# In-place activation sums on GpSimd, and three of seven out-projection products one step earlier, in a fused RWKV and feed-forward kernel

## The chip, the cores and the metric

The kernel runs on one core of a Trainium2 chip, in float32. The metric is the device time of one execution in microseconds (us), the median over repeated runs. The five engines run side by side, each through its own queue in order: TensorE (PE in the profile) multiplies matrices, VectorE (DVE) and ScalarE (ACT) compute element by element, GpSimd (POOL) does the same on data in SBUF, SyncE (SP) issues most DMAs. They wait for each other through semaphores.

## The reference

Two blocks in a row: a linear attention with a decaying state (RWKV-6), and a feed-forward layer with the activation h * erf(softplus(h)).

```python
def _attn_ref(r, k, v, w, u):                      # B, H, S, D = 4, 8, 768, 48
    for t in range(S):
        cur = np.einsum('bhd,bhe->bhde', u[None] * kt, vt)
        y[:, :, t] = np.einsum('bhd,bhde->bhe', rt, state + cur)
        state = wt[:, :, :, None] * state + np.einsum('bhd,bhe->bhde', kt, vt)

def _moe_ref(x, w_in, w_out):                      # 3072 x 384, 384 x 2048, 2048 x 384
    h = x @ w_in
    sp = np.maximum(h, 0.0) + np.log1p(np.exp(-np.abs(h)))
    g = h * erf(sp)
    return g @ w_out
```

The attention's output, with batch and sequence as tokens and the heads side by side, is the x of the second block.

## The kernel before

**Units and steps.** The 3072 tokens are cut into 12 units of 256: two batches by 128 positions. Units and steps are counted from 0, so unit 3 is the fourth. Step s does the attention of unit s, the hidden product (x @ w_in) of unit s - 1, the activation of units s - 1 and s - 2, and the out-projection (g @ w_out) of unit s - 3. After step 4 (DIRECT) the steps have one form, `attend_late`; steps 6 to 10 are alike. The last two units share a hidden product of another kind behind step 11.

**Hidden product.** `hidden` yields eight pieces a unit (L1123). A piece takes a PSUM tile from the pool ps_m, multiplies two blocks of 128 hidden features (three matmuls of 256 columns each), and ScalarE copies the tile to h (L1132). Two pieces make a chunk of the activation: softplus and erf on ScalarE (L1079, L1083), a multiplication in place on DVE (L1088).

**Out-projection.** A unit's activations are four quarters: a11 and a12 are the first batch's rows for the first and second half of the 2048 hidden features, a21 and a22 the second batch's. `project_fast` forms the product of this 2 x 2 block matrix and the equally cut w_out with seven products instead of eight (Winograd's form of Strassen's scheme). The sums of weights were made once. The sums of activations are s1 = a21 + a22, s2 = s1 - a11, s3 = a11 - a21, s4 = a12 - s2. `blend` makes them on DVE (L1222 to L1228), s3 in place of a21, the others into free room, and `to_lane` has ScalarE copy a22, a11 and a12 into PSUM first (L1203), so that DVE reads one operand from there. Each product is eight matmuls of 192 columns (L1245) into one of two PSUM tiles m0 and m1. These come from ps_m too, which has two buffers in all: while an out-projection is under way, no hidden piece can begin, and the first hidden piece behind it gets m0's buffer once all readers of m0 are done, the next m1's. The last reader of m0 is DVE's sum into both halves of o[1] (L1265), that of m1 DVE's sum into o[0] (L1270); then SP sends the outputs.

**Order.** The order on each engine is written out by hand. `attend_late` calls the stages front, near, 0, 1, 2, 3, 4 in between its own work, and each stage is a string of tokens: P one product of unit s - 3, Q one product of unit s - 2, H one hidden piece of unit s - 1, s and e one softplus and one erf, m one multiplication, F a part of the next unit's preparation, k a copy to PSUM, S a sum of activations. `LATE` holds the strings of steps 5 and 11, `USUAL` those of 6 to 10:

```python
USUAL = (
    "s P", "m", "ey P m s P P ep P", "m k22y P F P k11p F F", "S1", "S2 S3 H k12y S4 H F",
    "s H ey m H H F s H ep H H",
)
```

**Around it.** A step starts on PE with the own part of the unit before (L673) and one level of the present unit (L641); the stage front follows, then L673 and the part through the state (L699), whose result ScalarE copies and SP moves into xT (L707, L728, L734), the input of the next hidden product. Then `prepare(s + 1)` begins: POOL makes the totals of decays (L408, L430 to L432), a faded state (L802), and its share of the near part: totals L456, fading L463, products L504. DVE takes the rest: L485, L488, L494, L535, L538, the reductions L529, fadings L463. The two wait for each other several times; the first time DVE waits is at L488, for POOL's L463. The stages near and 0 come behind most of that on DVE's queue, so stage 0's multiplication (L1088), kT's scaling (L807) and everything behind them do too. PE's L641 of the last level and L761 stand between stages 0 and 1, the state's update (L748) between 1 and 2.

Of the kernel before, what the change touches and what calls it, by code (L numbers as in the profile page):

```python
# [11 lines left out]
FP32 = mybir.dt.float32  # L12
# [3 lines left out]
ALU = mybir.AluOpType  # L16

P = 128
FAST = 3
SEVEN = 1  # L20
EP = 64
HC = 64
NC = 2
NJ = 2
FG = 8
# [37 lines left out]
def kernel(  # L63
# [14 lines left out]
    nc = tc.nc  # L78
    PSUM = bass.MemoryType.PSUM

    n_steps, _, _, JP, C = rkw.shape
# [4 lines left out]
    _, NT, DM = w_out.shape  # L86
# [3 lines left out]
    SPC = NB // NJ  # L90
    assert C == P == NC * HC and HC == 1 << LOG and NE == 2 and D <= EP and NP * NE * D == DM == KT * P
    assert n_steps == SPC * n_pairs and NP == KT + 1 == 4 and NG == 2 and P // NEAR * NH == P
# [7 lines left out]
    outs = ctx.enter_context(tc.tile_pool(name="outs", bufs=2))  # L100
# [3 lines left out]
    ps_m = ctx.enter_context(tc.tile_pool(name="ps_m", bufs=2, space=PSUM))  # L104
# [19 lines left out]
    w_out_sb = const.tile([P, NT, DM], FP32, name="w_out_sb")  # L124
    ND = DM // NJ
    mixed = const.tile([P, 3, FG, ND], FP32, name="mixed")
# [7 lines left out]
    def products(shape, n=None):  # L134

        if n is None:
            n = turns["next"]
            turns["next"] = 1 - n
        names = "abc"[: len(shape) - 1]
        return banks[n][:].rearrange(  # L140
            f"p ({' '.join(names)}) -> p {' '.join(names)}", **dict(zip(names, shape[1:]))
        )
# [164 lines left out]
    def rows(e, n=D):  # L307
        return slice(e * EP, e * EP + n)

    both = slice(0, EP + D)  # L310

# [375 lines left out]
    def through_state(s, xT):  # L687
# [42 lines left out]
        for kk in range(KT):  # L730
            n = D // KT
            for e in range(NE):
                queue = nc.scalar if (kk, e) in by_scalar else nc.sync
                queue.dma_start(  # L734
                    out=xT[e * EP + D : (e + 1) * EP, kk, :],
                    in_=y3[e * EP + kk * n : e * EP + (kk + 1) * n, :],
                )
# [18 lines left out]
    def spread_blocks(s, pp):  # L756
# [3 lines left out]
        for e in range(NE):  # L760
            nc.tensor.matmul(  # L761
                pp[:EP, e, 0:2, HC // 2 : HC // 2 + n],
                lhsT=over_blocks[rows(e)].rearrange("p b n -> p (b n)"),
# [308 lines left out]
    def lane(kind):  # L1072

        if kind == "y":
            return y[:].rearrange("p e q j t -> p (e q j t)")
        return products([P, NE * JP * HC], 1)[:]

    def softplus_chunk():
        nc.scalar.activation(sp_room, chunks[0], AF.Softplus)  # L1079
# [6 lines left out]
    def multiply_chunk():  # L1086
        h, at = started.pop(0)
        nc.vector.tensor_mul(h, h, at)  # L1088
# [107 lines left out]
    def quarter(of, what):  # L1196

        g, j = int(what[1]) - 1, int(what[0]) - 1
        return gated[of][g][:, :, j * C : (j + 1) * C]

    def to_lane(of, what, kind):
        lanes[what] = lane(kind).rearrange("p (f t) -> p f t", t=C)
        nc.scalar.copy(lanes[what], quarter(of, what))  # L1203

    def blend(of, *parts):
# [14 lines left out]
        for part in parts or (1, 2, 4, 3):  # L1220
# [6 lines left out]
            else:  # L1227
                nc.vector.tensor_sub(s4, a["12"], s2)  # L1228

    def project_fast(s, gs):  # L1230

        c, i = divmod(s, SPC)
        a11, a12, a22 = gs[0][:, :, :C], gs[1][:, :, :C], gs[1][:, :, C:]
        s1, s2, s3, s4 = blends[s]
        upper, lower = w_out_sb[:, :FG], w_out_sb[:, FG:]
        b11, t1, b21, b22 = (x[:, :, k * ND : (k + 1) * ND] for x in (upper, lower) for k in range(2))
        t3, t2, t4 = (mixed[:, n] for n in range(3))
        o = [outs.tile([P, DM], FP32, name="o") for _ in range(NJ)]
        m0 = ps_m.tile([P, DM], FP32, name="m")
        m1 = ps_m.tile([P, DM], FP32, name="m")  # L1240
        lo, hi = slice(0, ND), slice(ND, DM)

        def product(to, a, b, start):
            for f in range(FG):
                nc.tensor.matmul(  # L1245
                    to, lhsT=a[:, f], rhs=b[:, f], start=start and f == 0, stop=f == FG - 1,
                    skip_group_check=True,
                )

        product(m0[:, lo], a11, b11, True)  # L1250
        nc.scalar.copy(o[0][:, lo], m0[:, lo])  # L1251
        yield
        product(m1[:, lo], a22, t4, True)
        yield
        product(m1[:, hi], s1, t1, False)
        nc.scalar.copy(o[1][:], m1[:])
        yield
        product(m0[:, lo], s2, t2, False)
        nc.scalar.copy(o[0][:, hi], m0[:, lo])
        yield  # L1260
        product(m1[:, hi], s4, b22, False)
        yield
        product(m0[:, lo], s3, t3, False)
        halves = o[1][:].rearrange("p (k n) -> p k n", k=2)
        nc.vector.tensor_add(halves, halves, m0[:, None, lo].to_broadcast([P, 2, ND]))  # L1265
        nc.sync.dma_start(out=out[i * NJ + 1, c], in_=o[1][:])
        yield
        if s < n_steps - 1:
            product(m1[:, lo], a12, b21, True)
            nc.vector.tensor_add(o[0][:], o[0][:], m1[:])  # L1270
            nc.sync.dma_start(out=out[i * NJ, c], in_=o[0][:])
        else:
            last = products([P, NE * JP * HC], 0)[:, lo]
            for part, m in ((hi, m1[:, hi]), (lo, last)):
                if m is last:
                    product(m, a12, b21, True)
                nc.vector.tensor_add(o[0][:, part], o[0][:, part], m)
                nc.sync.dma_start(out=out[i * NJ, c, :, part], in_=o[0][:, part])
        yield
# [113 lines left out]
    gated = [[] for _ in range(n_steps)]  # L1393

    def advance(count=None):

        while later and count != 0:
            stage, last = later.pop(0)
            stage()
            count = count and count - 1  # L1400
            if last and not count:
                break
# [10 lines left out]
    def piece(kind, of):  # L1413
        if not 0 <= of < n_steps:
            return
        if of not in kind:
            if kind is hids:
                kind[of] = hidden(of, xTs[of], gated[of], not of)
            else:
                kind[of] = (project_fast if of >= SEVEN else project)(of, gated[of])  # L1420
        next(kind[of])

    def in_order(s, k):
# [8 lines left out]
    STAGES_LATE = ("front", "near", 0, 1, 2, 3, 4)  # L1432
    LATE = {
        DIRECT + 1: (
            "s P", "m", "ey P m P s P ep P", "P m k22y F P k11p", "S1 F F",
            "S2 S3 H k12y S4 H F", "s H ey m H H F s H ep H H",
        ),
        n_steps - 1: (
            "s P", "m w", "ey P m s P P ep P", "m P P", "", "", ""
        ),  # L1440
    }
    USUAL = (
        "s P", "m", "ey P m s P P ep P", "m k22y P F P k11p F F", "S1", "S2 S3 H k12y S4 H F",
        "s H ey m H H F s H ep H H",
    )

    def run_late(s, tokens, following=None):

        for what in tokens.split():
            if what == "A":  # L1450
                advance()
            elif what == "P":
                piece(projs, s - 3)
            elif what == "H":
                piece(hids, s - 1)
            elif what == "F":
                next(following, None)
            elif what == "Q":
                piece(projs, s - 2)
            elif what == "J":  # L1460
                next(turns["joint"])
            elif what == "w":
                next(joining)
            elif what in "uvz":
                activate_pair(what)
            elif what == "T":
                join_tokens()
                turns["joint"] = hidden_of_two()
            elif what == "f":
                turns.pop("fill")()  # L1470
            elif what == "s":
                softplus_chunk()
            elif what[0] == "e":
                erf_chunk(what[1])
            elif what == "m":
                multiply_chunk()
            elif what[0] == "k":
                to_lane(s - 2, what[1:3], what[3])
            else:
                blend(s - 2, *(int(n) for n in what[1:]))  # L1480
                for name in {"S3": ("11", "22"), "S4": ("12",)}.get(what, ()):
                    lanes.pop(name, None)
# [24 lines left out]
    for kk in range(KT):  # L1507
        n = D // KT
        to, of = (x.rearrange("p (e m) -> p e m", e=NE) for x in (apart[:, kk], ident[:]))
        nc.vector.tensor_copy(out=to[:, :, D:], in_=of[:, :, kk * n : (kk + 1) * n])  # L1510
    load_first()
    with tc.manual_schedule(
# [78 lines left out]
        s = n_steps  # L1591
        from_own(s - 1, ready[s - 1][0], 1)
        fence()
        run_late(s - 1, "S Q w w w")
        from_own(s - 1, ready[s - 1][0], 0)
        through_state(s - 1, xTs[s - 1])
        run_late(s, "P P P P T")
        run_late(s, "J J J J J u J u u J")
        run_late(s, "J u v J J v J z z J v v J z u u u J z")
        run_late(s, "J u v J J v J z z J v v J z u u J z")  # L1600
        run_late(s, "J J u v J J z v J z v J z u v J z P P S s ey")
        run_late(s + 1, "P P m s ep P P m P P P S")
        run_late(s + 2, "P P P P P P P")

# [95 lines left out]
```

## Time and profile before

| What | us |
|---|---|
| median of three runs (575.89 to 577.66) | 576.53 |
| span of the profiled execution, first to last instruction | 575.4 |
| from one step's start to the next, steps 6 to 9 | 44.3 |
| of it the hidden product on PE | 20.9 |
| DVE busy in such a step | 37.1 |
| ScalarE busy in such a step | 29.2 |
| GpSimd busy in such a step | 22.6 |

The span is that of one execution taken by the profiler; the runs' times are taken around the whole launch. A row of the timeline gives the start and the duration in us, the engine, the source line, the operation, the tile written and those read, the shape and how many instructions are merged; in brackets, how long the engine had been idle and who released it. A float32 matmul shows as two records, so eight matmuls are x16. Busy matmuls overlap in the records, so PE's pace is read from start to start.

### The profile page before, as it was taken

Reading aid. Unit: us, or ns where it says so; the run is one execution under the profiler, and the core shown is the slowest. Engines: PE = TensorE matmul, PEld = TensorE weight load, DVE = VectorE, ACT = ScalarE, POOL = GpSimd, SP = SyncE. Lnnn points to the kernel's source line nnn. Section 1 sums busy time; section 2 is a strip of 40 time slices with the busy share of each in tenths; the row PEclk is TensorE's granted clock in tenths of the full one; section 3 lists DMA queues with packets and bytes.
Section 4 is the critical chain, followed back from the end, with each engine's and each line's share of the span. In section 5 each row is a group of like instructions: output and inputs, shape, how many; then the busy total and the mean of one; then the engine's idle time right before and its main releaser. Section 6 shows DMA issues by size and latency. Waiting matters only on the chain.

```text
span 575.4 us, 16716 instructions
## 1 busy us (share of the span) xinstructions
PE 568.1 (99%) x7336; PEld 503.9 (88%) x7336; DVE 442.7 (77%) x475; ACT 358.0 (62%) x488; POOL 244.7 (43%) x265
## 2 busy tenths in 40 slices
PE   8999999999999999999999999999999999999997
PEld 6688777678998998998998998998898899988997
DVE  7785887999899998798699699599599527255640
ACT  3668777645458858748747756766766661388700
POOL 4567381632885883393384284185173000000000
PEclk9999999999999999999999999999999999999999
DMA  7595662350435325155145145234232201000000
GB/s 263 192 348 214 240 205 68 161 164 3 147 84 168 109 66 171 21 176 166 18 159 167 32 145 172 40 121 162 39 120 74 48 8 37 1 1 2 27 28 27
DMA packets 54081, 63.24 MB, mean 110 GB/s; under 512 B 35160, under 2 KB 40568, under 8 KB 52984
## 3 DMA queue, kind: packets, MB, share of 16 engines
q1 hardware_dynamic: 53624, 61.98, 34.0%
q8 instruction: 57, 0.93, 0.7%
q10 hardware_dynamic: 384, 0.20, 0.1%
q14 instruction: 16, 0.13, 0.1%
HBM read 52.39 MB, written 8.69 MB: 106 GB/s over the span
## 4 chain that ended last, share of the span: by engine, by line
PE 93%; DVE 4%; ACT 2%; issue 1%; POOL 0%; DVEq 0%; ACTq 0%; POOLq 0%
PE m L1245 34%; PE m L1123 33%; PE pp L641 5%; PE pp L1333 4%; PE m L1155 4%; PE y L1333 2%; PE y L673 2%; PE y L699 2%; PE pp L748 2%; PE m L951 1%; DVE in L334 1%; PE pp L960 1%; PE pp L1033 1%; DVE h L1088 1%; ACT rest L267 0%
## 5 line engine op out<-in xcount | busy, mean ns | idle before, releaser
L1123 PE MATMUL m<-xT,w_in_sb 128*128 128x256 f32 x960 | 215.0, 382 | 0.9 <-ACT h L1132 0.7
L1123 PEld LDWEIGHTS m<-xT,w_in_sb 128*128 128x128 f32 x960 | 179.8, 190 | 26.5 <-ACT h L1132 1.4
L334 DVE TENSOR_TENSOR in<-in,tot_sb 128x1024 f32<-128x1024 f32 (+1 forms) x55 | 80.1, 1457 | 12.7 <-PE pp L641 11.4
L1132 ACT COPY h<-m 128x512 f32<-128x512 f32 x80 | 46.1, 580 | 48.5 <-PE m L1123 48.4
L1245 PE MATMUL m<-mixed,h 128*128 128x192 f32 x320 | 56.7, 331 | 0.0
L1245 PE MATMUL m<-w_out_sb,h 128*128 128x192 f32 x320 | 56.2, 329 | 0.0
L1245 PEld LDWEIGHTS m<-mixed,h 128*128 128x128 f32 x320 | 51.8, 190 | 1.0
L1245 PE MATMUL m<-w_out_sb,room 128*128 128x192 f32 x304 | 52.5, 326 | 0.0
L1245 PEld LDWEIGHTS m<-w_out_sb,h 128*128 128x128 f32 x320 | 52.0, 190 | 0.5
L1245 PEld LDWEIGHTS m<-w_out_sb,room 128*128 128x128 f32 x304 | 49.9, 190 | 0.0
L1083 ACT ACT_TABLE_LOAD x30 | 38.5, 1283 | 10.7 <-DVE h L1088 8.5
L463 POOL TENSOR_TENSOR words<-words,own 128x384 f32<-128x384 f32 x21 | 30.1, 1432 | 22.8 <-DVE words L494 13.0
L504 POOL TENSOR_TENSOR words<-words 128x384 f32<-128x384 f32 x28 | 39.7, 1447 | 0.0
L1079 ACT ACT_TABLE_LOAD x30 | 38.5, 1283 | 1.8 <-issue 1.3
L641 PEld LDWEIGHTS pp<-in 48*48 48x48 f32 (+4 forms) x2368 | 30.1, 120 | 10.8 <-issue 3.5
L456 POOL TENSOR_TENSOR own<-rest 128x384 f32<-128x384 f32 x7 | 9.7, 1379 | 61.0 <-ACT o L1251 61.0
L641 PE MATMUL pp<-in 48*48 48x32 f32 (+4 forms) x2368 | 33.9, 206 | 0.2 <-DVE in L334 0.2
L504 POOL TENSOR_TENSOR rk<-words 128x384 f32<-128x384 f32 x28 | 33.4, 1220 | 0.0
L529 DVE TENSOR_REDUCE sums<-rk 128x16 f32<-128x768 f32 (+2 forms) x31 | 31.6, 1020 | 0.0
L408 POOL TENSOR_TENSOR tot_sb<-tot_sb 128x256 f32<-128x256 f32 (+4 forms) x50 | 28.8, 576 | 3.8
L1079 ACT ACTIVATE room<-h 128x1024 f32<-128x1024 f32 x28 | 29.6, 1057 | 0.3
L1245 PE MATMUL m<-mixed,room 128*128 128x192 f32 x160 | 27.7, 327 | 0.0
(206 smaller groups left out, 981.6 us busy)
## 6 DMA issues: line engine op xcount, KB each, us to landing
in<-in_rkw SPq DMA_DIRECT2D x8, 1024.0 KB, 5.2
words<-in_moe_w_in SPq DMA_DIRECT2D x16, 384.0 KB, 5.4
words<-in_moe_w_out SPq DMA_DIRECT2D x16, 384.0 KB, 5.2
words<-in_rk_rows SPq DMA_DIRECT2D x8, 768.0 KB, 6.1
w<-in_rkw SPq DMA_DIRECT2D x11, 512.0 KB
v<-in_v SPq DMA_DIRECT2D x12, 384.0 KB, 5.6
out<-o SPq DMA_DIRECT2D x23, 192.0 KB, 3.0
in<-in_rkw SPq DMA_DIRECT2D x7, 512.0 KB, 5.6
```

The source lines that it names most:

```text
L334: nc.vector.tensor_mul(halves, halves, view(tots[level - 1], 0, [[1, n], [2, nb], [0, half]]))
L408: nc.gpsimd.tensor_mul(new, pair[:, :, 0], pair[:, :, 1])
L463: engine.tensor_mul(to, to, of[:, :, None, :].to_broadcast([P, NEAR // 2 // half, half, D]))
L504: engine.tensor_mul(to[:, i], r[:, half:], k[:, part * rows + i, None].to_broadcast([P, half, D]),)
L529: nc.vector.tensor_reduce(out=to, in_=of, axis=mybir.AxisListType.X, op=ALU.add)
L641: nc.tensor.matmul(to, lhsT=rk(1, n)[rows(e), s0 : s0 + m], rhs=right, start=True, stop=True,)
L1079: nc.scalar.activation(sp_room, chunks[0], AF.Softplus)
L1083: nc.scalar.activation(at, sp_room, AF.Erf)
L1123: nc.tensor.matmul(ps[:, ff, :], lhsT=w_in_sb[:, g * FG + f + ff, kk * P : (kk + 1) * P], rhs=xT[:, kk, :], start=kk == 0, stop=kk == KT - 1,)
L1132: nc.scalar.copy(h[:, f : f + FT, :], ps[:])
L1245: nc.tensor.matmul(to, lhsT=a[:, f], rhs=b[:, f], start=start and f == 0, stop=f == FG - 1, skip_group_check=True,)
L1333: nc.tensor.matmul(to[:, e], lhsT=a[:, 2 * i + e], rhs=b, start=start and not k, stop=True, skip_group_check=True,)
```

## The change

A new function `project_placed` takes the place of `project_fast` for units 3 to 9 (the last two keep the old form), with a new order of the seven products and another grouping of the same sums. The four sums of activations are made by GpSimd, each in place of a quarter that no later product needs (`blend_placed`, token I). The copies to PSUM (token k) and DVE's sums (token S) go from these units. The first three products (a11, a22, a12 as they are) become tokens Q at the end of the step before, the other four stay in the stages front and 0. The hidden pieces move the other way: one to the end of stage 0, two into stage 1. Steps 5 and 11 and the tail are fitted to it.

```diff
+    def blend_placed(of, part):
+        a11, a12, a21, a22 = (quarter(of, what) for what in ("11", "12", "21", "22"))
+        out_, a, b, op = {
+            3: (a21, a11, a21, ALU.subtract), 2: (a22, a22, a21, ALU.subtract),
+            1: (a11, a11, a22, ALU.add), 4: (a12, a12, a22, ALU.subtract),
+        }[part]
+        nc.gpsimd.tensor_tensor(out=out_, in0=a, in1=b, op=op)
+
+    def project_placed(s, gs):
...
+        product(m0[:, lo], a11, b11, True)
+        nc.scalar.copy(o[0][:, lo], m0[:, lo])
+        yield
+        product(m1[:, lo], a22, t4, True)
+        yield
+        product(m1[:, hi], a12, b21, False)
+        nc.scalar.copy(o[1][:, lo], m1[:, lo])
+        nc.vector.tensor_add(o[0][:, lo], o[0][:, lo], m1[:, hi])
+        yield
+        product(m0[:, lo], a22, t2, False)
+        nc.scalar.copy(o[0][:, hi], m0[:, lo])
+        yield
+        product(m1[:, lo], a11, t1, True)
+        nc.scalar.copy(o[1][:, hi], m1[:, lo])
+        yield
+        product(m0[:, lo], a21, t3, False)
+        halves = o[1][:].rearrange("p (k n) -> p k n", k=2)
+        nc.vector.tensor_add(halves, halves, m0[:, None, lo].to_broadcast([P, 2, ND]))
+        nc.sync.dma_start(out=out[i * NJ + 1, c], in_=o[1][:])
+        yield
+        product(m1[:, lo], a12, b22, False)
+        nc.vector.tensor_add(o[0][:, hi], o[0][:, hi], m1[:, lo])
+        nc.sync.dma_start(out=out[i * NJ, c], in_=o[0][:])
+        yield
...
     LATE = {
         DIRECT + 1: (
-            "s P", "m", "ey P m P s P ep P", "P m k22y F P k11p", "S1 F F",
-            "S2 S3 H k12y S4 H F", "s H ey m H H F s H ep H H",
+            "s P", "m", "ey P m P s P ep P", "P m F P", "I3 F F",
+            "H H F", "s H ey m H H F s H ep H H Q Q I2 Q I1 I4",
         ),
         n_steps - 1: (
-            "s P", "m w", "ey P m s P P ep P", "m P P", "", "", ""
+            "s P", "m w", "ey P m s P ep P", "m I3 Q Q I2", "", "", ""
         ),
     }
     USUAL = (
-        "s P", "m", "ey P m s P P ep P", "m k22y P F P k11p F F", "S1", "S2 S3 H k12y S4 H F",
-        "s H ey m H H F s H ep H H",
+        "s P", "m", "ey P m s P P ep H", "m H F H F F", "I3", "H H F",
+        "s H ey m H H F s Q ep Q I2 Q I1 I4",
     )
...
-        run_late(s - 1, "S Q w w w")
+        run_late(s - 1, "Q I1 I4 w w w")
         from_own(s - 1, ready[s - 1][0], 0)
         through_state(s - 1, xTs[s - 1])
-        run_late(s, "P P P P T")
+        run_late(s, "P P P T")
...
-        run_late(s, "J J u J J z v J z v J z u v J z P P S s ey")
+        run_late(s, "J J u J J z v J z v J z u v J z P S s ey")
```

More of the change, by code (lines that the diff above doesn't have):

```diff
@@ L20 @@
 SEVEN = 1
+PLACED = 3
 EP = 64
@@ L1228, in blend, with product @@
                 nc.vector.tensor_sub(s4, a["12"], s2)
+    def blend_placed(of, part):
[6 more added lines that the diff above has]
+    def project_placed(s, gs):
+        c, i = divmod(s, SPC)
+        a11, a12, a21, a22 = (quarter(s, what) for what in ("11", "12", "21", "22"))
+        upper, lower = w_out_sb[:, :FG], w_out_sb[:, FG:]
+        b11, t1, b21, b22 = (x[:, :, k * ND : (k + 1) * ND] for x in (upper, lower) for k in range(2))
+        t3, t2, t4 = (mixed[:, n] for n in range(3))
+        o = [outs.tile([P, DM], FP32, name="o") for _ in range(NJ)]
+        m0 = ps_m.tile([P, DM], FP32, name="m")
+        m1 = ps_m.tile([P, DM], FP32, name="m")
+        lo, hi = slice(0, ND), slice(ND, DM)
+        def product(to, a, b, start):
+            for f in range(FG):
+                nc.tensor.matmul(
+                    to, lhsT=a[:, f], rhs=b[:, f], start=start and f == 0, stop=f == FG - 1,
+                    skip_group_check=True,
+                )
+        product(m0[:, lo], a11, b11, True)
[22 more added lines that the diff above has]
+        yield
     def project_fast(s, gs):
@@ L1419, in piece @@
             else:
-                kind[of] = (project_fast if of >= SEVEN else project)(of, gated[of])
+                kind[of] = (
+                    project if of < SEVEN
+                    else project_placed if PLACED <= of < n_steps - 2
+                    else project_fast
+                )(of, gated[of])
         next(kind[of])
@@ L1478, in run_late @@
                 to_lane(s - 2, what[1:3], what[3])
+            elif what[0] == "I":
+                blend_placed(s - 2, int(what[1]))
             else:
@@ L1600 @@
         run_late(s, "J u v J J v J z z J v v J z u u J z")
-        run_late(s, "J J u v J J z v J z v J z u v J z P P S s ey")
+        run_late(s, "J J u v J J z v J z v J z u v J z P S s ey")
         run_late(s + 1, "P P m s ep P P m P P P S")
```

## The prediction

> **What bounds the kernel now.** I read the page's busy shares first, then what TensorE (PE) waits for, then one late step instruction by instruction on PE, VectorE (DVE) and GpSimd (POOL). The page says that PE is the busy engine:
>
> ```profile
> PE 568.1 (99%) x7336; PEld 503.9 (88%) x7336; DVE 442.7 (77%) x475; ACT 358.0 (62%) x488; POOL 244.7 (43%) x265
> ```
>
> The list of PE's waits has only two entries over 0.6 us (engine, line, releaser, total, times, longest), one before the first matmul and one for ScalarE's copies of the hidden products:
>
> ```profile
> PE m L951 <- POOL ident masks.py:199: 1.7, 1, 1.7
> PE m L1123 <- ACT h L1132: 0.7, 2, 0.3
> ```
>
> From about 50 us on PE stops once, for 0.35 us at 224.4, and a late step is exactly as long as its matmuls. PE's timeline of the step that begins at 365.63 (start, duration, instruction):
>
> ```profile
> 365.63 0.66 PE L673 MATMUL y<-own,v 64*48 64x64 f32 x32
> ...
> 371.21 2.87 PE L1245 MATMUL m<-mixed,h 128*128 128x192 f32 x16
> 373.92 2.76 PE L1245 MATMUL m<-w_out_sb,room 128*128 128x192 f32 x16
> 376.52 2.76 PE L1245 MATMUL m<-mixed,room 128*128 128x192 f32 x16
> 379.12 2.76 PE L1245 MATMUL m<-w_out_sb,room 128*128 128x192 f32 x16
> ```
>
> The step before began at 321.33: the period is 44.30 us. I count from a step's start, t = 0 at 365.63. An out-projection product is 2.60 to 2.71 us. A piece of the hidden product is 2.62 (96 records in 20.99 us, eight pieces). There is no slack on PE: every wait that the change puts into its queue is paid in full, and nothing on another engine can be won.
>
> **What it takes away.** Per unit four DVE sums (1.21 us each) and three ScalarE copies (1.02) go. Both lie wholly under PE's 44.30 us, so they are worth 0. The one wait that they cause, the 0.35 us in step 5 (a copy of the hidden product stands behind them on ScalarE), may go: -0.35 us. PE's work stays seven products a unit. The smaller copies out of PSUM (ScalarE two of 192 columns for one of 384, DVE one of 192 more) are 0.3 us each on engines with room: 0. The same two output DMAs are issued per unit, some 2 us earlier in the step: 0.
>
> **What it moves.** With three products at the end of the step before, a usual step (6 to 10) has only four left, and the first piece of the next hidden product (token H at the end of stage 0) follows them. PE's order is then: the first of the four from 1.30, the other three from 371.21 - 365.63 = 5.58, and after three products (2.71 + 2.60 + 2.60) PE is at the hidden piece at t = 13.5. That piece takes a PSUM tile from ps_m, which has two buffers, both held by the out-projection's m0 and m1. It needs m0, and m0 is free only when DVE has added it into o[1] (the sum of both halves, L1265). Its other need, xT, is in time: SP begins its six issues at t = 6.4 (372.02), 0.58 us each by the median, and the slowest DMA of that line lands 2.8 us after its issue: 12.7 at the latest. Now DVE's timeline of the same step:
>
> ```profile
> 373.26 1.03 DVE L488 TENSOR_TENSOR rk<-words 128x384 f32<-128x384 f32 x2 [0.42 <-POOL words L463]
> ...
> 383.46 1.21 DVE L1088 TENSOR_TENSOR h<-h,y 128x1024 f32<-128x1024 f32 x1
> 384.59 1.32 DVE L334 TENSOR_TENSOR in<-in,tot_sb 128x512 f32<-128x512 f32 x1
> 385.83 1.21 DVE L1088 TENSOR_TENSOR h<-h,pp 128x1024 f32<-128x1024 f32 x1
> 386.96 0.54 DVE L1265 TENSOR_TENSOR o<-o,m 128x384 f32<-128x384 f32 x1
> ```
>
> The new order puts that sum right behind the multiplication at 383.46 (token m of stage 0), so in the place of the L334 at 384.59, t = 18.96. All of DVE's work ahead of it, the next unit's preparation, stays; the four sums taken away stood behind this place. Even with nothing else late, the sum ends at 18.96 + 0.54 = 19.5 and PE stands still from 13.5: 6.0 us a step.
>
> **What it adds.** POOL gets four sums of 128x1024 per unit, which the trace does not have on POOL. The nearest row is a subtraction in place on the same kind of strided view, 128x1536 in 3442 ns, so 2.24 ns per element and 2.29 us a sum:
>
> ```profile
> L1186 POOL TENSOR_TENSOR w_out_sb<-w_out_sb x1: 3442/3442/3442, 123.4 to 123.4; 128x1536 f32<-128x1536 f32 x1
> ```
>
> From below, L830 (834 ns for 384 elements, 2.17) gives 2.22; from above, L456 beside busy DVE (1.41 us for 384, 3.67) gives 3.76. I take 2.29. Sum 3 stands in stage 2, ahead of L830, where POOL idles 2.76 us for DVE today: its 2.29 is hidden there, and would delay only the state's sum, which no matmul needs before the next step. Sum 2 overwrites a22 and so waits for the second moved product, whose end is one product (2.60) before the next step's start; sums 1 and 4 follow. They end at t = -2.60 + 3 x 2.29 = 4.3. What is queued behind them on POOL is the next unit's preparation:
>
> ```profile
> 350.98 1.04 POOL L408 TENSOR_TENSOR tot_sb<-w 128x512 f32<-128x512 f32 x1
> 352.10 2.07 POOL L408 TENSOR_TENSOR tot_sb<-tot_sb 128x256 f32<-128x256 f32 x5
> 354.12 0.25 POOL L430 TENSOR_TENSOR over_blocks<-tot_sb 128x16 f32<-128x16 f32 x1
> ...
> 357.24 0.83 POOL L802 TENSOR_TENSOR faded<-s,tot_sb 128x384 f32<-128x384 f32 x1 [2.58 <-DVE s L833]
> 370.55 1.41 POOL L456 TENSOR_TENSOR own<-rest 128x384 f32<-128x384 f32 x1 [12.48 <-ACT o L1251]
> 371.92 1.31 POOL L463 TENSOR_TENSOR words<-words,rest 128x384 f32<-128x384 f32 x1
> ```
>
> Today POOL does the totals (L408 to L432, 350.98 to 354.67) a whole half step ahead and then idles 12.48 us, until L456 can start at t = 4.92. After the change totals and L802 stand behind sum 4: 4.3 + 3.14 + 0.55 + 0.83 = 8.8 at L456, + 1.37 + 1.31 = 11.5 at the end of L463. DVE's L488 waits for that L463 (it started at t = 7.63), so it comes 3.9 us later. From L488 to the place of the sum DVE needs 384.59 - 373.26 = 11.33 us, without a pause: the sum ends at 11.5 + 11.33 + 0.54 = 23.4. PE's stall: 23.4 - 13.5 = 9.9 us. The next pieces wait for nothing more (m1's sum is 0.3 us behind), the other DVE and POOL work ends well before the stretched step does, and so the next step begins in the same state.
>
> **The clock.** A pause of 10 us is new here; the longest after the start is 0.41 us and costs no clock. At the start of the trace, where PE comes from standing still, the first matmuls have doubled durations:
>
> ```profile
> L951 PE MATMUL m<-ident x20: 379/634/792, 1.7 to 10.2; 128*128 128x256 f32 x20
> ```
>
> Twelve passes at 0.40 us start to start instead of 0.22 (20.99 / 96): 2.2 us lost. Bounds for a pause of 10 us: 0 (as after 0.41) and 2.2 (as at the start). I take 2.2, since 10 us is nearer to standing still. [...]
>
> **The sum.** Five steps have this order (6 to 10). Step 5 still has all seven products of unit 2 ahead of its hidden pieces, and step 11 has no preparation and no hidden piece behind its products. In the tail one product instead of two stands ahead of the sums of unit 10, but PE still has 2 x 2.60 us of that unit ahead and the first sum takes 1.2: 0. So 5 x (9.9 + 2.2) - 0.35 = 60.2. On the profile's 575.4 us span that is 635.6; the median of the runs lies 1.1 above the span, so 637.
>
> **The rivals.**
> (a) No half clock after the stall: 5 x 9.9 - 0.35 = 49, 626. For it: the page's granted clock reads full throughout. Against: it reads full over the doubled matmuls of the start too, so I go by durations; no pause in mid-run is long enough to tell.
> (b) POOL's lateness stays hidden and only DVE's order counts: 5 x (6.0 + 2.2) = 41, 617. It needs sum 4 to end by t = 0.4 instead of 4.3, that is sums of 1.0 us; no POOL row is that fast.
> (c) POOL's sums run at the rate of L456 beside DVE, 3.76 us: they end at 8.7, the stall is 14.3, 5 x (14.3 + 2.2) = 82.5, 659. For it: sums 1 and 4 lie beside DVE's L334 and L535 to L538; and a DVE multiplication L463 took 1.24 us beside POOL's L456 against 0.56 otherwise. Against: DVE stops at L488 by t = 7.2 and leaves POOL alone. [...]
> (d) Not slower: the hidden piece finds m0 free. The place is L1265's successor on DVE, the point from which it decides is its end by t = 13.5, 9.9 us earlier than worked out. Then all waits vanish under PE and the time is 576 (the 0.35 us won). It would need the preparation on DVE and POOL ahead of the sum to shrink to half, and nothing of it is removed.
>
> **Chances.** Forecast 0.62, (a) 0.17, (b) 0.06, (c) 0.11, (d) 0.04. A measurement here tells 0.3% (1.7 us) from no change. (d) alone is not slower: same 0.03, faster 0.01, slower 0.96. The range takes in (a) and (b) and reaches most of the way to (c): 614 to 655.
>
> **What would show it.** In steps 6 to 10 PE idle of about 10 us ahead of the hidden product, put down to DVE's sum o<-o,m; then a stretch of hidden matmuls with doubled durations and a period near 56.4 us. POOL's totals behind the in-place sums, each 2.2 to 2.5 us; DVE waiting 3 to 5 us for POOL at L488. No stall in step 5 and in the tail. A hidden piece that starts at t = 13.5 would prove the forecast wrong, a stall of 6 us its POOL part.

## The result, and the profile after

The changed kernel takes 646.38 us (median of 4 runs, 645.5 to 648.85), the one before 576.9 beside it: a ratio of 1.1215, 95% interval 1.1195 to 1.1235. It is 69.5 us slower. The profiled execution is the slowest of the four (648.85, span 647.0; the others have spans of 643.7 to 645.4); some 2 us of it lie in waits before 50 us, where both kernels do the same.

The page of the changed kernel, busy times and the granted clock over 40 slices:

```profile
PE 578.1 (89%) x7336; PEld 510.2 (79%) x7336; DVE 424.6 (66%) x454; ACT 342.6 (53%) x477; POOL 314.2 (49%) x293
...
PEclk9999999999999999599779969997997999999999
```

PE has the same 7336 matmul records, 10 us more busy time and 69 us of idle time (7 before). The clock row (PEclk, the clock granted to PE in tenths of full speed), flat before, has five dips. The list of PE's waits (line waited on, total, times, longest) names one cause that was not there before:

```profile
PE m L1124 <- DVE o L1277: 60.4, 5, 12.1
```

L1124 is the hidden product and L1277 DVE's sum out of m0, in the new line numbers. Five times 12.1 us: one stall in each of steps 6 to 10. Step 7 begins at 300.25. PE's timeline of it shows the last product of the four, and then the first hidden piece:

```profile
300.25 0.67 PE L674 MATMUL y<-own,v 64*48 64x64 f32 x32
...
311.14 2.76 PE L1255 MATMUL m<-w_out_sb,h 128*128 128x192 f32 x16
325.98 4.93 PE L1124 MATMUL m<-xT,w_in_sb 128*128 128x256 f32 x12 [12.07 <-DVE o L1277]
330.84 0.76 PE L642 MATMUL pp<-in 48*32 48x32 f32 x64
```

PE could start the piece at 313.9, t = 13.7, and starts it at t = 25.7. The piece then takes 4.86 us to the next instruction instead of 2.62, and the five steps' periods are 58.1 to 59.3 us instead of 44.3. POOL's timeline around the same step's start:

```profile
297.89 8.09 POOL L1238 TENSOR_TENSOR h<-h 128x1024 f32<-128x1024 f32 x3 [16.91 <-PE m L1255]
305.94 1.75 POOL L409 TENSOR_TENSOR tot_sb<-w 128x512 f32<-128x512 f32 x1
307.77 3.07 POOL L409 TENSOR_TENSOR tot_sb<-tot_sb 128x256 f32<-128x256 f32 x5
...
312.09 1.01 POOL L457 TENSOR_TENSOR own<-rest 128x384 f32<-128x384 f32 x1
313.05 1.01 POOL L464 TENSOR_TENSOR words<-words,rest 128x384 f32<-128x384 f32 x1
```

The three in-place sums come first, because sum 2 must wait for the second moved product (16.91 us of idle time); the totals, done half a step ahead in the old kernel, stand behind them. And DVE:

```profile
301.69 2.07 DVE L335 TENSOR_TENSOR in<-in,tot_sb 128x1024 f32<-128x1024 f32 x1 [0.54 <-PE pp L642]
...
304.30 2.50 DVE L536 TENSOR_TENSOR rk<-words,u_row 128x768 f32<-128x768 f32 x1
...
314.08 1.03 DVE L489 TENSOR_TENSOR rk<-words 128x384 f32<-128x384 f32 x2 [3.55 <-POOL words L464]
...
324.25 1.21 DVE L1089 TENSOR_TENSOR h<-h,y 128x1024 f32<-128x1024 f32 x1
325.38 0.54 DVE L1277 TENSOR_TENSOR o<-o,m 128x384 f32<-128x384 f32 x1
```

L489 (L488 before) waits 3.55 us for POOL's L464 and starts at t = 13.8 instead of 7.6; from there to the sum DVE runs without a pause, as before, and 0.06 us after the sum's end PE goes on. Last, the clock during and after the stall of step 6 (stretch, length, PE busy and its instructions, granted clock, DMA share, GB/s):

```profile
254.50:266.60 12.10, 0.12 (x1) 0.67 0.17 70
266.60:272.00 5.40, 5.31 (x12) 0.50 0.20 73
```

While PE stands still the granted clock falls to half: in step 6 it reads 1.00 up to 258.5, 0.53 from there to 259.0, 4 us after the last product, and 0.50 to the stall's end, so that the mean over the stall is 0.67. In step 7 it reads 0.78 over 316 to 317 already, some 2.7 us after the last product. The whole first hidden piece of step 6 runs at 0.50.

### The profile page after: what moved, and what is told of

It reads as the page before. It is cut to its first block, busy times and chain, and to the rows that moved or that the text cites. A ratio compares the mean times of both kernels' runs of the same rounds, so it can differ in the third digit from the quotient of the medians.

```text
span 647.0 us, 16744 instructions
## 1 busy us (share of the span) xinstructions
PE 578.1 (89%) x7336; PEld 510.2 (79%) x7336; DVE 424.6 (66%) x454; ACT 342.6 (53%) x477; POOL 314.2 (49%) x293
## 4 chain that ended last, share of the span: by engine, by line
PE 75%; POOL 12%; DVE 9%; DMA 1%; issue 1%; ACT 0%; SPq 0%; POOLq 0%; DVEq 0%; ACTq 0%
PE m L1124 33%; PE m L1300 11%; PE m L1255 11%; POOL h L1238 5%; PE pp L642 4%; PE pp L1388 4%; PE m L1156 3%; POOL tot_sb L409 3%; DVE sums L530 2%; PE y L1388 2%; DVE h L1089 2%; DVE words L495 2%; PE pp L749 2%; POOL words L464 2%; PE y L674 1%
## 5 line engine op out<-in xcount | busy, mean ns | idle before, releaser
L1124 PE MATMUL m<-xT,w_in_sb 128*128 128x256 f32 x960 | 226.8, 394 | 61.6 <-DVE o L1277 60.4
L1124 PEld LDWEIGHTS m<-xT,w_in_sb 128*128 128x128 f32 x960 | 185.6, 197 | 90.5 <-DVE o L1277 61.9
L1238 POOL TENSOR_TENSOR h<-h 128x1024 f32<-128x1024 f32 x28 | 74.3, 2665 | 118.1 <-PE m L1255 117.6
L335 DVE TENSOR_TENSOR in<-in,tot_sb 128x1024 f32<-128x1024 f32 (+1 forms) x55 | 78.9, 1436 | 33.3 <-PE pp L642 31.7
L1255 PE MATMUL m<-w_out_sb,h 128*128 128x192 f32 x448 | 78.2, 328 | 0.0
L1255 PEld LDWEIGHTS m<-w_out_sb,h 128*128 128x128 f32 x448 | 73.3, 190 | 1.0
L1089 DVE TENSOR_TENSOR h<-h,y 128x1024 f32<-128x1024 f32 x13 | 15.8, 1215 | 36.1 <-ACT y L1084 36.1
L464 POOL TENSOR_TENSOR words<-words,own 128x384 f32<-128x384 f32 x21 | 26.6, 1267 | 22.7 <-DVE words L495 13.0
L409 POOL TENSOR_TENSOR tot_sb<-tot_sb 128x256 f32<-128x256 f32 (+4 forms) x50 | 33.8, 677 | 3.8
L1267 DVE TENSOR_TENSOR o<-o,m 128x192 f32<-128x192 f32 x7 | 2.5, 354 | 48.5 <-ACT o L1266 48.5
L505 POOL TENSOR_TENSOR words<-words 128x384 f32<-128x384 f32 x28 | 32.4, 1187 | 0.0
L290 POOL TENSOR_TENSOR w_out_sb<-w_out_sb,rest 128x768 int32<-128x768 int32 x8 | 18.1, 2256 | 20.9 <-DVE w_out_sb L282 20.8
```

The costliest lines, as they stand in the source:

```text
L335: nc.vector.tensor_mul(halves, halves, view(tots[level - 1], 0, [[1, n], [2, nb], [0, half]]))
L409: nc.gpsimd.tensor_mul(new, pair[:, :, 0], pair[:, :, 1])
L464: engine.tensor_mul(to, to, of[:, :, None, :].to_broadcast([P, NEAR // 2 // half, half, D]))
L505: engine.tensor_mul(to[:, i], r[:, half:], k[:, part * rows + i, None].to_broadcast([P, half, D]),)
L1124: nc.tensor.matmul(ps[:, ff, :], lhsT=w_in_sb[:, g * FG + f + ff, kk * P : (kk + 1) * P], rhs=xT[:, kk, :], start=kk == 0, stop=kk == KT - 1,)
L1238: nc.gpsimd.tensor_tensor(out=out_, in0=a, in1=b, op=op)
```

## The experiments

My theory had one stall with two causes that add up, and a cost on top. DVE's sum of m0 stands behind the preparation in DVE's queue (6 us). POOL's sums make that preparation late (the rest). And the stall costs PE its clock.

**No sums at all.** The four sums of units 3 to 9 are left out of the computation, so POOL is free again.

```diff
             elif what[0] == "I":
-                blend_placed(s - 2, int(what[1]))
+                pass
```

> The changed kernel without the four in-place sums of units 3 to 9 (they are left out of the computation), everything else as it is. Theory (two delays in one stall: DVE's sum of m0 stands behind the preparation, 6.0 us, and POOL's sums make the preparation itself late, the other 6 us): PE's stall ahead of the hidden piece falls from 12.1 to about 6.0 us, the clock loss stays near 2 us, 5 x 8 = 40 over before, about 617. Rival A (POOL's lateness alone makes the stall, DVE's order has room): no stall, about 577. Rival B (the moved products or the hidden input make PE wait, not the sums): unchanged, about 646.

Measured: 618.53 us, against 576.29 of the kernel before on that chip. PE's waits:

```profile
PE m L1124 <- DVE o L1277: 29.5, 5, 5.9
```

And DVE's timeline, in a step that begins at 290.78:

```profile
294.84 0.55 DVE L486 TENSOR_TENSOR rk<-words 128x384 f32<-128x384 f32 x1
...
298.43 1.03 DVE L489 TENSOR_TENSOR rk<-words 128x384 f32<-128x384 f32 x2 [0.43 <-POOL words L464]
...
309.74 0.54 DVE L1277 TENSOR_TENSOR o<-o,m 128x384 f32<-128x384 f32 x1
```

DVE is back at its old pace (L489 at t = 7.65), and still the sum comes at t = 19.0 and PE waits 5.9 us. So the order on DVE alone costs 42 us, with its share of the clock, and POOL's sums the other 27 (69.5 - 42.2). Both rivals fall.

**The sums on DVE.** The same in-place sums, and the same new order.

```diff
-        nc.gpsimd.tensor_tensor(out=out_, in0=a, in1=b, op=op)
+        nc.vector.tensor_tensor(out=out_, in0=a, in1=b, op=op)
```

> The changed kernel with the same in-place sums on DVE instead of POOL. Theory: POOL starts the totals half a step ahead again, DVE's share of the preparation runs at its old durations (L536 0.94 us instead of 2.50), DVE pays three sums of about 1.2 us at the end of a step where it idles, so the stall is 6.0 to 7 us, with the clock's 2 us about 618 to 622. Rival A (only the amount of elementwise work ahead of DVE's sum counts, wherever it runs): stall as before or longer, 646 or more. Rival B (DVE's order has room once POOL is free): 577.

Measured: 627.15 us, stalls of 7.6 to 7.8 us. The theory's side, but 5 us over its range. DVE's timeline around a step's start at 293.08 says why:

```profile
290.59 1.23 DVE L1238 TENSOR_TENSOR h<-h 128x1024 f32<-128x1024 f32 x1 [3.67 <-PE m L1255]
293.54 0.36 DVE L1267 TENSOR_TENSOR o<-o,m 128x192 f32<-128x192 f32 x1 [1.73 <-ACT o L1266]
293.81 2.35 DVE L1238 TENSOR_TENSOR h<-h 128x1024 f32<-128x1024 f32 x2
296.08 0.17 DVE L683 COPY seen<-y 128x16 f32<-128x16 f32 x1
```

Sums 1 and 4 (the x2) do not run in DVE's pause at the end of the step: the sum L1267 stands ahead of them and waits for ScalarE's copy (L1266) behind the third product. They take 2.3 us of the next step's start instead.

**PE kept busy.** Sixteen matmuls of zeros in front of the first hidden piece.

```diff
-        "s P", "m", "ey P m s P P ep H", "m H F H F F", "I3", "H H F",
+        "s P", "m", "ey P m s P P ep W H", "m H F H F F", "I3", "H H F",
...
+            elif what == "W":
+                keep_busy(products([P, NE, JP, HC], 0), (DM,) * 16)
```

> The changed kernel with 16 matmuls of zeros (384 columns, 0.65 us each, about 10.4 us) put on PE ahead of the first hidden piece of steps 6 to 10, into a bank that is free there. Theory (the hidden matmuls behind the stall run at half clock because PE stood idle): they run at 0.22 us a pass again, the first piece takes 2.6 instead of 4.3 to 5.4 us, the stall's end does not move, and the time falls by about 10 us to 636. Rival (they are slow for another reason, for instance operands that come late): first piece as slow as now, time 646 or more.

Measured: 638.06 us. PE's timeline (L1125 is L1124 of the changed kernel, one line on):

```profile
310.25 10.48 PE L962 MATMUL pp<-s,ident 128*128 128x384 f32 x32
322.52 2.86 PE L1125 MATMUL m<-xT,w_in_sb 128*128 128x256 f32 x12 [1.78 <-DVE o L1278]
325.30 0.76 PE L643 MATMUL pp<-in 48*32 48x32 f32 x64
```

The piece takes its normal 2.78 us to the next instruction, the granted clock is full throughout (mean 1.000 instead of 0.955), and the stall ends where it did (t = 25.8). The time falls by 8 us where 10 were expected; the period falls to 56.7 us, 9 us over the five steps. So the matmuls behind the stall are slow where PE stood idle ahead of them; the zeros lie in the stall and do not move its end.

**ScalarE takes m0 and m1 out.** Steps 6 to 11 copy the last contents of m0 and m1 to free room at once; DVE adds later.

```diff
+        u0, u1 = (room[:, n, :ND] for n in (2, 3))
+        nc.scalar.copy(u0, m0[:, lo])
-        nc.vector.tensor_add(halves, halves, m0[:, None, lo].to_broadcast([P, 2, ND]))
+        nc.vector.tensor_add(halves, halves, u0[:, None].to_broadcast([P, 2, ND]))
...
+        nc.scalar.copy(u1, m1[:, lo])
-        nc.vector.tensor_add(o[0][:, hi], o[0][:, hi], m1[:, lo])
+        nc.vector.tensor_add(o[0][:, hi], o[0][:, hi], u1)
```

> The changed kernel, but in steps 6 to 11 ScalarE copies the last results in m0 and m1 to free room at once, and DVE adds from there. Theory (the first hidden piece waits for m0's last reader, DVE's sum): the first piece starts at t = 13.6 without a wait; the next limit is ScalarE, which has the erf that waits for DVE's multiplication (t = 21) ahead of the first piece's copy, so that the third piece waits until about t = 24 instead of 19.7: some 5 us a step and less clock loss, about 602 to 610. Rival (the piece waits for something else, the hidden input or the buffer of h): the stall of 12 us stays ahead of the first piece, 646.

Measured: 610.41 us, just past the upper end of what was expected. The wait in front of the first piece is gone, and the next one is where it was expected, at the third piece. First PE, then ScalarE in the same step, which begins at 289.73:

```profile
303.22 2.75 PE L1124 MATMUL m<-xT,w_in_sb 128*128 128x256 f32 x12
...
313.90 4.54 PE L1124 MATMUL m<-xT,w_in_sb 128*128 128x256 f32 x12 [4.21 <-ACT h L1133]
```

```profile
311.01 1.28 ACT L1084 ACT_TABLE_LOAD   x1 [7.27 <-DVE h L1089]
312.31 1.03 ACT L1084 ACTIVATE pp<-room 128x1024 f32<-128x1024 f32 x1
313.27 0.58 ACT L1133 COPY h<-m 128x512 f32<-128x512 f32 x1
```

The first piece starts at t = 13.5. The copy of its result stands behind an erf that waits 7.27 us for DVE's late multiplication, and the third piece needs its buffer.

**The hidden pieces back in stage 3.**

```diff
-        "s P", "m", "ey P m s P P ep H", "m H F H F F", "I3", "H H F",
+        "s P", "m", "ey P m s P P ep", "m F F F", "I3", "H H H H H F",
```

> The changed kernel with the three early hidden pieces of steps 6 to 10 put back into stage 3, behind the state's update; the three products stay a step ahead. Theory (with three products gone from the front of the step PE runs ahead of DVE's preparation, and any work that needs DVE stops it): the wait moves to the state's update, which needs kT (DVE ends it at t = 24), and then m0's sum at t = 25.7; the stall is 12.1 less the 1.8 us of PE work that now stands ahead, about 10.3 in two parts, about 636 to 640. Rival (the early hidden pieces are the mistake): no stall, 577.

Measured: 637.73 us. PE's waits:

```profile
PE pp L749 <- ACT own L659: 51.4, 5, 10.3
```

The size is the expected one, in one piece: the state's update starts at t = 24.85 (320.47 in a step from 295.62). The releaser is not kT itself but ScalarE's copies (L659), which stand behind the same erf that waits for DVE. So the early pieces are not the mistake by themselves: the state's update, now the next work there, waits for DVE as well, by way of ScalarE.

**POOL's sums in the old order.** The kernel before, with `blend` on POOL for units 3 to 8 and without the tokens k.

```diff
+        engine = nc.gpsimd if FAST <= of < n_steps - 3 else nc.vector
-                nc.vector.tensor_add(s1, s3, a["22"])
+                engine.tensor_add(s1, s3, a["22"])
...
-        "s P", "m", "ey P m s P P ep P", "m k22y P F P k11p F F", "S1", "S2 S3 H k12y S4 H F",
+        "s P", "m", "ey P m s P P ep P", "m P F P F F", "S1", "S2 S3 H S4 H F",
```

> The kernel before with the old order of products and pieces, its activation sums of units 3 to 8 made by POOL in stages 2 and 3 (into the old rooms, without the copies to PSUM). Theory (POOL's sums cost only where they stand ahead of the preparation's totals): four sums of 2.35 us fit into the 12.5 us that POOL idles, the totals are done before the step ends, no stall: 576 to 577. Rival (POOL's sums slow DVE wherever they run, through the SBUF they share): some of the 12 us a step comes back, 585 or more.

Measured: 577.25 us against 577.62, ratio 0.9995 (0.9978 to 1.0012). POOL's timeline:

```profile
307.13 2.36 POOL L1225 TENSOR_TENSOR room<-room,h 128x1024 f32<-128x1024 f32 x1
...
320.37 0.83 POOL L802 TENSOR_TENSOR faded<-s,tot_sb 128x384 f32<-128x384 f32 x1
327.00 1.41 POOL L456 TENSOR_TENSOR own<-rest 128x384 f32<-128x384 f32 x1 [5.80 <-ACT o L1252]
```

The sums are as long as in the changed kernel, the totals behind them are done, and POOL still idles 5.80 us ahead of L456. POOL's sums cost nothing there, and the work taken from DVE and ScalarE gains nothing.

**Copy-out with the erf behind the pieces.** ScalarE's copies of m0 and m1 stay as above; the erf that waits for DVE now stands behind three hidden pieces.

```diff
-        "s P", "m", "ey P m s P P ep H", "m H F H F F", "I3", "H H F",
+        "s P", "m", "ey P m s P P H", "H H ep m F F F", "I3", "H H F",
```

> The copy-out of m0 and m1 by ScalarE as before, and in steps 6 to 10 the erf that waits for DVE issued behind the second and third hidden piece (both moved up to stage 1's start). POOL's sums stay. Theory: neither piece waits; what is left is the state's update, which needs kT from DVE at t = 24 instead of 22.4, 1.6 us a step without loss of clock: about 584. Rival (ScalarE was not what made the third piece wait): still 4 us and half clock, about 605.

Measured: 592.94 us. No piece waits any more; the state's update does, five times (1.6 to 2.8 us, 12.0 in all), as expected, but for 2.5 us instead of 1.6 in most steps. PE's timeline:

```profile
310.00 1.53 PE L749 MATMUL pp<-v,kT 64*48 64x48 f32 x64 [2.51 <-issue]
```

It starts 0.1 us after DVE has ended kT (308.59 + 1.31), which is at t = 25 instead of the expected 24. POOL made it later: its L464 ends at t = 14.7 instead of the 13.8 of the changed kernel, and DVE waits 3.54 us for it at L489. DVE and POOL around this step's start at 284.94:

```profile
284.05 1.95 DVE L604 TENSOR_TENSOR own<-block_sb,by_tokens 128x1024 f32<-128x1024 f32 x1 [2.23 <-DMA by_tokens<-by_blocks]
285.00 3.22 POOL L1238 TENSOR_TENSOR h<-h 128x1024 f32<-128x1024 f32 x1
```

In the changed kernel L604 ran before POOL's sums, in 1.22 us. Here it waits for a DMA until sum 2 is under way, and sum 1, next on POOL, takes 3.22 us instead of 2.35: it ends 2.2 us behind L604's end. The clock was lost too, in two of the five steps (the state's update takes 1.53 and 1.46 us there, 0.94 in the first step). The expected size was 9 us too small.

**Copy-out, erf behind, sums on DVE.** The last version together with `nc.vector` in `blend_placed`.

> The same with the in-place sums on DVE, so that POOL is on time. Theory (the two causes add up and nothing else is behind the loss): kT is done by t = 19.5, no stall is left, the time is that of before, 576 to 577, with the three products still a step ahead. Rival (the moved products cost PE time by themselves, for instance through more changes of weights or a hidden third wait): 580 or more.

Measured: 577.09 us against 577.62, ratio 0.9998 (0.9983 to 1.0013). PE's busy time is 566.8 of a span of 574.5 us, and its longest wait past the start is one of 0.8 us, none in a late step. With both causes out, and the erf behind the pieces, the three products a step ahead cost nothing and bring nothing. No version tried beats the kernel before.

## Why the prediction was right, point by point

- **What bounds the kernel:** right. PE has no slack, so each wait is paid, and work taken from DVE and ScalarE is worth nothing (the old order with POOL's sums, at 0.9995 of the time of before).
- **The place of DVE's sum, 6.0 us:** right, 5.9 without the sums.
- **POOL's lateness, 3.9 us:** right in kind, too small: the whole stall is 12.1 us instead of 9.9, and this term holds the difference. Step by step: sums 2 and 1 took 2.35 us (2.29 taken), but sum 4 took 3.34 and ended 2.2 us behind DVE's L335; sum 2 began 0.24 us later than taken; the totals took 5.36 us instead of 3.69 beside DVE's next operations (L536, L486, L539); L803 to L464 were 0.75 faster (2.76 instead of 3.51), with DVE waiting. Together L464 ends at t = 13.8 instead of 11.5, and the stall is 2.2 us longer. I took the price of an undisturbed row for work that I had seen lie beside DVE's two-input operations, and kept the disturbed one for rival (c) alone. Five times 2.2 is 11 us, where the forecast and the median are 9 apart.
- **The chain from L488 to the sum, 11.33 us:** 11.30.
- **The half clock, 2.2 us a stall:** right on average, 2.06 (first pieces of 5.41, 4.86, 4.52, 4.35 and 4.25 us to the next instruction instead of 2.62). With the matmuls of zeros in the idle time the piece took 2.78 us and the granted clock was 1.000 instead of 0.955. The length of the pause, by which I chose between the bounds, did not decide the size: pauses of 4.2 us cost as much (1.7 to 2.6 us each), and two pauses of 2.5 us cost the clock as well.
- **Step 5 and the tail:** right. Step 5's pause of 0.35 us is gone, and there is no stall behind step 10.
- **The rivals:** (a) fell with the dips of the clock row and the slow pieces behind them, (b) with the 12.1 us, (d) with the stall itself. (c) had the cause of the missing 9 us, POOL's sums longer beside DVE, but at twice its size (a stall of 14.3 us): of the three sums only sum 4 took longer, 3.34 us, and the totals behind it were slow only until DVE stopped at L489, from 310.5 on.

## What to carry to other kernels

When one engine is full, ask of a reordering only what it puts in that engine's way. Moving work off the engines around it gained nothing here (0.9995 of the time of before), and moving the full engine's own work earlier only made it reach the next dependency sooner (0.9998 with both causes out). A buffer that two kinds of work share ties the first use of the one to the last reader of the other, wherever that reader stands in its own queue: 12.1 us a step here. And on an engine that idles half the time, an operation costs what is queued behind it: the same four sums of a unit were free half a step earlier, where POOL still idled behind them, and cost 27 us where the preparation stood behind them.

## What the runs showed of the hardware

- **POOL and DVE side by side.** Three of DVE's operations on two SBUF operands took longer beside POOL's sums and totals than without them: 2.50 us instead of 0.94 (L536), 1.39 instead of 0.55 (L486), 2.07 instead of 1.23 (L335). Starts and ends in step 7 say more. Sum 1 began at 300.32 and took 2.36 us, as sum 2 did with DVE idle (2.35), though L335 started at 301.69; L335 ended 1.1 us behind it. Then came sum 4:

```profile
302.64 3.34 POOL L1238 TENSOR_TENSOR h<-h 128x1024 f32<-128x1024 f32 x1
```

It ended 2.2 us after L335's end, and L536, started at 304.30, ended 0.8 us after sum 4's. So L335, sum 4 and L536 each ended a little less than their undisturbed time (1.23, 2.35 and 0.94 us) after the other engine's operation; why, no run shows. DVE's L1267, which reads one operand from PSUM, took 0.35 us beside sum 1, and 0.36 in the version with the sums on DVE.

- **Two pauses of 2.5 us cost the clock.** After 4.2 us of idle time the piece behind it was slow in all five steps of the first copy-out (4.31 to 5.18 us to the next instruction instead of 2.62). With the erf behind the pieces, the pause of 1.6 us cost no clock (1.00 from 261.5 to 270), but of the four of 2.5 to 2.8 us two did (both of 2.51; those of 2.52 and 2.78 did not), for instance this one (the pause and what follows, columns as above):

```profile
307.50:310.00 2.50, 0.00 (x0) 0.95 0.00 0
310.00:312.00 2.00, 2.00 (x65) 0.50 0.04 8
```

- **The loss did not grow with the pause.** The first piece behind it lost 1.7 to 2.6 us after 4.2 us of idle time, 1.7 to 2.8 after 5.9 and 1.6 to 2.8 after 12.1.
